# An order of steps for each unit, joint sums of h, and one add moved to GpSimd, in a fused attention and expert kernel

## The chip, the cores and the metric

The kernel runs on one core of one Trainium2 chip. The core has five engines with a queue of instructions each: TensorE (PE; its weight loads are shown as PEld) multiplies matrices and writes to PSUM, eight banks of 512 float32 words in each of 128 partitions; VectorE (DVE), ScalarE (ACT) and GpSimd (POOL) do elementwise work, and SyncE (SP) issues DMAs. Each queue is worked off in order, and engines wait for one another by semaphores. The metric is the device time of one execution in microseconds (us), as the median of several.

## The reference

What is computed is a linear attention with exponential features, whose output is the input of eight experts with a balanced, dense routing:

```python
def phi(x):
    proj = np.einsum('bhsd,df->bhsf', x, w_phi)
    proj = proj - np.max(np.abs(proj), axis=-1, keepdims=True)
    return np.concatenate([np.exp(proj), np.exp(-proj)], axis=-1)
q_p, k_p = phi(q), phi(k)                      # q, k, v: 8 x 8 x 576 x 64
kv = np.einsum('bhsf,bhsd->bhfd', k_p, v)
num = np.einsum('bhsf,bhfd->bhsd', q_p, kv)
den = np.einsum('bhsf,bhf->bhs', q_p, np.sum(k_p, axis=2))[..., None] + 1e-06
x = (num / den), heads side by side            # 4608 x 512
P = routing(x @ w_gate)                        # 4608 x 8, eight rounds of normalising
out = sum over e of P[:, e:e+1] * (relu(x @ w1[e]) @ w2[e])   # w1: 512 x 1024, w2: 1024 x 512
```

All inputs and the output are float32; the kernel multiplies in bfloat16.

## The kernel before

**Stages.** Attention comes first, with the up and down products of expert 0 mixed into it and into the routing, to 244 us. Then come the experts 1 to 7 (`for e in range(1, E)`, near the end of the function), then a short end with the last down products.

**Groups, pairs, units.** The 4608 tokens are nine groups of 512 (g = 0 to 8); groups 0 and 1, 2 and 3, and so on form pairs, group 8 is single. For each expert the loop runs over the four pairs and the single group (in expert 7 the single one first), and for a pair over two halves of the hidden features (fp = 0, 1). Each round of this inner loop is a unit: nine to an expert. A unit has an up part (x @ w1 and relu, of its own groups) and a down part (h @ w2) of one group whose h was completed earlier. An h of a group is two tiles H[0], H[1], one from each fp, which lie in one of six slots of the tile `hs`. The downs lag behind: a pair is complete after its fp = 1 unit, its first group's down is part of the next unit, and its second group's down part of the one after that.

**Products of Strassen's kind.** Up and down are 2 x 2 block products done with seven multiplications (`up7`, `down7`), so sums of blocks have to be made on DVE: `sums_up` and `sums_down` for the weights, `sums_x` for x (kept in DRAM and loaded again for each expert), and in `down7` four sums of the h blocks of each fp, 512 elements a partition each (`sub`, L1239). They go to the tiles S0, S1, S2 (buffers `hx`), and one in place into h. Steps X1, Y1, Z1, X2, X3, Z2, X4 are the seven down products, eight matmuls of 256 columns each (L1462). Their results are scaled by P and added to `acc`, by DVE from PSUM (L1840) or by ACT into a tile V (L1852) and then GpSimd (L1855).

**Fine products.** In experts 2 to 7 the pairs' up part is `up49`: two of its seven products, y (block 12 of w1 with block 21 of x: product two) and w, are themselves done with seven multiplications (`fine`, L1603), in steps a, b, c, d and k. Step a copies one partial product to a tile m5 (kept in xT, ACT, L1615); step b adds m5 to a second partial product (DVE, L1624); the last function, `last` (L1638), adds m5 to the second half of bank 1. For y this add is made in place in PSUM, at the start of step yk, and then `add` (L1664, with relu) forms two blocks of h from y's two banks and k1, the float32 copy of product x1 (ACT `keep`, L1660).

**The order of the work.** A unit's steps are called in the order of a list: `EARLY` for the pairs of expert 1, `FINE[2]` for a single group, and for fine units `FINE[0]` (fp = 1), `FINE[1]` (fp = 0 of an expert's first pair) or `FINE[3]` (other fp = 0). The lists are priorities only: each step calls `pe`, `act`, `dve`, `pool` or `dma`, which enter an operation in a plan. `Plan.schedule` then simulates all engines with costs of its own and takes, each time, the operation that can start first, and of equal ones the one entered first; the queues of the chip get this order. GpSimd's operations and those of DVE marked `shared` (the sums) never overlap in the plan, and a GpSimd operation planned shortly behind such a DVE one gets a wait for it.

**Loads.** X blocks for a pair are loaded by `load_fine` (L1393, SP's queue), into six places for plain blocks and four for fine ones, used in turn; a load waits until the last matmul that reads the place is done. In expert 7 the stores of the output go through the same queue.

Of the kernel before, what the change touches and what calls it, by code (L numbers as in the profile page):

```python
# [12 lines left out]
ALU = mybir.AluOpType  # L13
# [336 lines left out]
def kernel(  # L350
# [650 lines left out]
    def akey(g):  # L1001
        return ["late"] * (g >= NA) + ["P"] * (g >= 9)
# [568 lines left out]
    def up49(A, fp, X, H, gs, r0):  # L1571
# [16 lines left out]
        def fine(bank, an, xn, more=(), takes=(), wk=(), out_c=None):  # L1588

            f, r = A[an]  # L1590
            s, rs = A[an + "*"]
            t, rt = X[xn]
            r = r + rs + rt + list(r0)
            m5, key, first = M5.next()

            def a(q, k):
                return lambda: f()[:, k, 128 * (2 * fp + q):][:, 0:128]

            def sf(n):
                return lambda: s()[:, n, fp, :]  # L1600

            def mul(q, n, lhs, rhs, more=(), takes=(), start=False, wk=()):
                pe(256, lambda: nc.tensor.matmul(  # L1603
                    halves_of(bank[q], n)(), lhsT=lhs(), rhs=t()[:, rhs, :], start=start,
                    stop=True, skip_group_check=True), r + list(more), [bank[q], *wk], takes)

            def copy(q, n, q2, n2):
                act(293, lambda: nc.scalar.copy(
                    out=halves_of(bank[q], n)(), in_=halves_of(bank[q2], n2)()),
                    [bank[q2]], [bank[q]])  # L1610

            def a1():
                mul(1, 0, sf(0), 3, more, takes, True, wk)
                mul(1, 1, a(0, 0), 0)
                act(256, lambda: nc.scalar.copy(out=m5(), in_=halves_of(bank[1], 0)()),  # L1615
                    [bank[1]], [key, *first])
                act(293, lambda: nc.scalar.copy(
                    out=halves_of(bank[0], 0)(), in_=halves_of(bank[1], 1)()),
                    [bank[1]], [bank[0]])

            def a2():
                mul(1, 1, sf(1), 4)
                mul(0, 0, a(0, 1), 1)
                dve(256, lambda: nc.vector.tensor_tensor(  # L1624
                    out=halves_of(bank[0], 1)(), in0=halves_of(bank[1], 1)(), in1=m5(),
                    op=ALU.add), [bank[1], key], [bank[0]])

            def a3():
                mul(1, 1, sf(2), 5)
                mul(0, 1, sf(3), 2)  # L1630
                if out_c is None:
                    copy(1, 0, 1, 1)

            def a4():
                mul(1, 0, a(1, 1), 6, start=out_c is not None)

            def last(out_=None, w=None):
                dve(256, lambda: nc.vector.tensor_tensor(  # L1638
                    out=out_() if out_ else halves_of(bank[1], 1)(),
                    in0=halves_of(bank[1], 1)(), in1=m5(), op=ALU.add),  # L1640
                    [bank[1], key] if out_ else [key], [w] if out_ else [bank[1]])

            return a1, a2, a3, a4, last
# [63 lines left out]
                        [y[q]])  # L1707

        def yk():
            ys[4]()  # L1710
            for q in range(2):
                add(y, q, k1, 1, 1)

# [66 lines left out]
    def down7(e, g, H, B7):  # L1780
# [5 lines left out]
        def hk(i, j, fps=(0, 1)):  # L1786
            return [(H[fp], q, j, i) for fp in fps for q in range(2)]

        late, seen = akey(g), set()
        S = [new(f"S{i}") for i in range(3)]  # L1790
        for fp in range(2):
            def h(i, j, fp=fp):
                return lambda: H[fp]()[:, j, :, 256 * i:256 * i + 256]

            def s(n, fp=fp):
                return lambda: S[n]()[:, 2 * fp:2 * fp + 2]

            f = (fp,)
            end0 = ["dn0"] if e == 1 else []
            sub(dve, 512, s(0), h(1, 0), h(1, 1), ALU.add, hk(1, 0, f) + hk(1, 1, f) + end0,  # L1800
                [(S[0], fp)])
            sub(dve, 512, h(1, 0), h(0, 0), h(1, 0), ALU.subtract, hk(0, 0, f), hk(1, 0, f))
            sub(dve, 512, s(1), s(0), h(0, 0), ALU.subtract,
                [(S[0], fp)] + hk(0, 0, f), [(S[1], fp)])
            sub(dve, 512, s(2), h(0, 1), s(1), ALU.subtract,
                [(S[1], fp)] + hk(0, 1, f), [(S[2], fp)])

        def sk(n):
            return [(S[n], fp) for fp in range(2)]
# [4 lines left out]
        def prod(bank, lhs, y, r, first, more=(), wk=()):  # L1814
            f, r2 = B7[y]
            product(bank, lambda k, i: lhs(k)[:, 128 * i:128 * i + 128],
                    lambda k: f()[:, k, :], 4, r + r2 + (["P"] if e else late) + list(more), first,
                    wk=wk)

        def start(bank, i, j):  # L1820

            out_ = acc_part(g, i, j)
            w = [("acc", g, 2 * i + n, j) for n in range(2)]
            if (i, j) in seen:
                dve(515, lambda: nc.vector.tensor_tensor(
                    out=out_(), in0=bank().rearrange("p (a b) -> p a b", a=2), in1=out_(),
                    op=ALU.add), [bank] + late, w)
            else:
                act(512, lambda: nc.scalar.copy(
                    out=out_(), in_=bank().rearrange("p (a b) -> p a b", a=2)),  # L1830
                    [bank] + late, w)
            seen.add((i, j))

        def read(bank, i, j):
# [62 lines left out]
        def stores():  # L1897
            if e == E - 1:
# [3 lines left out]
        return {"out": stores, "X1": X1, "Y1": Y1, "Z1": Z1, "X2": X2, "X3": X3, "Z2": Z2, "X4": X4}  # L1902


    EARLY = ("X1 x10 w10 x11 X2 x20 y10 x21 Z1 y11 X3 w11 x30 x31 x40 x41 w20 Y1 w21 X4 Z2").split()
    END = "X1 p2 Y1 X2 Z1 p3 X3 Z2 X4 p0 p1".split()
    FINE = [("x11 wa X1 wb wc Z1 X2 wd x10 Z2 ya wk yb x20 x30 yc x21 x31 X3 yd yk w21 x40 x41 Y1 X4 "
             "w20").split(),
            ("X1 ya yb Z1 X2 x11 wa yc wb Z2 X3 Y1 wc wd x10 yd X4 x20 wk x21 yk x30 x31 w20 x40 x41 "
             "w21").split(),  # L1910
            ("x11 y11 x10 x21 w11 Z1 X1 X2 y10 w10 x31 X3 x20 w21 Y1 X4 x41 x30 x40 w20 Z2").split(),
            ("wa wb x11 wc Z1 X1 x10 ya yb yc Z2 x20 wd X2 yd wk X3 x30 yk w20 x21 x40 x31 X4 Y1 w21 "
             "x41").split()]
    slots, wait = list(range(6)), []

    def take():
# [18 lines left out]
    for e in range(1, E):  # L1935
        w1, w2 = load_w(e, ["late", ("acc", 4, 0, 0)] if e > 1 else ["late"])
        if e == 1:
            nextX = sums_x(pairs[0])
        A7 = sums_up(e, w1)
        B7 = sums_down(e, w2) if e > 1 else None  # L1940
        turn = [*pairs, (8,)] if e < E - 1 else [(8,), *pairs]
        if e == 2:
            o = plan.op("X", 0.0, 0.0, lambda: None, w=["K"])
            for d in plan.ops[:-1]:
                if any(b.ring is R["X"] for b in d.bufs):
                    d.users.append(o)
                    o.deps.append(d)
                    o.left += 1
        for n, gs in enumerate(turn):
            if (e, n) == (1, 4):  # L1950
                plan.inorder = 1
            X = nextX if e == 1 else load_fine(gs)
            H = {g: [] for g in gs}
            for fp in range(len(gs)):
                hs = take()
                for i, z in enumerate(hs):
                    H[gs[min(i, len(gs) - 1)]].append(z)
                fine = e > 1 and len(gs) == 2
                if fine:
                    un = up49(A7, fp, X, H, gs, ["up0", "K"])  # L1960
                else:
                    un = up7(A7, gs, fp, X, H, ["up0"])
                single = (e, n) >= (1, 4)
                for o in (FINE[fp == 0 and (1 if n == (e == E - 1) else 3)] if fine else FINE[2] if single else
                          EARLY):
                    if o in un:
                        un[o]()
                    elif len(o) == 3:
                        un[o[:2], int(o[2])]()
                    elif dn is not None:  # L1970
                        dn[o]()
                if dn is not None:
                    dn["out"]()
                    slots.extend(dn["slots"])
                if e == 1 and fp == 0 and n + 1 < len(turn):
                    nextX = sums_x(turn[n + 1], [(H[gs[0]][0], 0, 1, 1)])
                if B7 is None and fp:
                    B7 = sums_down(e, w2)
                if fp == len(gs) - 1:
                    wait += [(e, g, H[g], B7, w2, [z.ring.number for z in H[g]]) for g in gs]  # L1980
                dn = next_down()
# [35 lines left out]
```

## Time and profile before

| | |
|---|---|
| median of 3 runs | 1015.81 us (1015.67 to 1017.01) |
| profiled execution | 1017.14 us, span 1015.4 us |
| PE busy | 999.9 us (98%) |
| PEld busy | 714.1 us (70%) |
| DVE busy | 905.2 us (89%) |
| ACT busy | 770.3 us (76%) |
| POOL busy | 379.6 us (37%) |

The span goes from the first to the last instruction of the profiled execution; its own time has 1.7 us more around that. A busy time is the union of the recorded spans of an engine's instructions, waits not counted. Lines such as L1239 are lines of the kernel, and where a helper makes the instruction it is the helper's line. Rows of groups give the operation, output and inputs by the program's names, shapes, count, then busy time, mean duration, and the idle time before them with what ended it.

### The profile page before, as it was taken

Reading aid. Unit: us, or ns where it says so; the run is one execution under the profiler, and the core shown is the slowest. Engines: PE = TensorE matmul, PEld = TensorE weight load, DVE = VectorE, ACT = ScalarE, POOL = GpSimd, SP = SyncE. Lnnn points to the kernel's source line nnn. Section 1 sums busy time; section 2 is a strip of 40 time slices with the busy share of each in tenths; the row PEclk is TensorE's granted clock in tenths of the full one; section 3 lists DMA queues with packets and bytes.
Section 4 is the critical chain, followed back from the end, with each engine's and each line's share of the span. In section 5 each row is a group of like instructions: output and inputs, shape, how many; then the busy total and the mean of one; then the engine's idle time right before and its main releaser. Section 6 shows DMA issues by size and latency. Waiting matters only on the chain.

```text
span 1015.4 us, 22774 instructions
## 1 busy us (share of the span) xinstructions
PE 999.9 (98%) x8232; PEld 714.1 (70%) x8232; DVE 905.2 (89%) x2075; ACT 770.3 (76%) x1786; POOL 379.6 (37%) x418
## 2 busy tenths in 40 slices
PE   7899999999999999999999999999999999999998
PEld 5666666644576867787777777787778777887775
DVE  7999988987888898999989999899989999988896
ACT  7999999836988777777777677767776777667773
POOL 5778764400123323242333323333342223333323
PEclk9999999999999999999999999999999999999999
DMA  9999999181132622283326333452228222625453
GB/s 251 187 194 184 164 149 132 38 171 47 68 111 74 185 88 89 66 182 100 104 68 143 98 99 98 81 148 89 89 73 203 89 89 66 138 89 150 158 178 125
DMA packets 129681, 123.33 MB, mean 121 GB/s; under 512 B 55712, under 2 KB 98720, under 8 KB 129568
## 3 DMA queue, kind: packets, MB, share of 16 engines
q1 hardware_dynamic: 97616, 97.82, 34.5%
q0 software_dynamic: 31648, 23.86, 16.9%
q8 instruction: 64, 1.05, 0.4%
q14 instruction: 49, 0.40, 0.1%
q10 hardware_dynamic: 304, 0.20, 0.1%
HBM read 117.78 MB, written 18.74 MB: 134 GB/s over the span
## 4 chain that ended last, share of the span: by engine, by line
PE 93%; ACT 3%; DVE 2%; DMA 1%; issue 1%; DVEq 0%; ACTq 0%
PE ps L1462 41%; PE ps L1471 24%; PE ps L621 18%; PE ps L1603 7%; PE ps L904 2%; ACT k L617 1%; DMA xT<-wx 1%; ACT q L617 1%; DMA xT<-xp 0%; ACT acc L1862 0%; DVE m L613 0%; DVE wx L613 0%; PE ps L751 0%; DMA acc<-in_k_dram 0%; PE ps L933 0%
## 5 line engine op out<-in xcount | busy, mean ns | idle before, releaser
L1855 POOL TENSOR_TENSOR acc<-acc,hx 128x512 f32<-128x512 f32 x186 | 235.7, 1271 | 557.9 <-ACT hx L1852 264.9
L1462 PEld LDWEIGHTS <-hs 128*128 128x128 bf16 x1984 | 194.0, 98 | 57.5 <-issue 1.1
L1840 DVE SCALAR_TENSOR_TENSOR acc<-ps,P,acc 128x256 f32<-128x256 f32 x372 | 162.0, 478 | 45.8 <-PE ps L1462 28.5
L1852 ACT ACTIVATE hx<-ps,P 128x256 f32<-128x256 f32 x372 | 156.7, 477 | 48.1 <-PE ps L1462 44.7
L1471 PE MATMUL ps<-xT,T 128*128 128x512 bf16 x608 | 175.8, 379 | 0.8 <-DMA xT<-xp 0.8
L1462 PEld LDWEIGHTS <-hx 128*128 128x128 bf16 x1488 | 145.6, 98 | 27.4 <-issue 0.3
L1462 PE MATMUL ps<-hx,hs 128*128 128x256 bf16 x992 | 141.1, 273 | 0.6 <-ACT hx L1852 0.4
L1664 DVE CUSTOM_DVE_ANT_0 hs<-ps,U 128x512 bf16<-128x512 f32 x192 | 128.7, 683 | 3.5 <-PE ps L1462 1.5
L1471 PEld LDWEIGHTS <-T 128*128 128x128 bf16 x672 | 65.8, 98 | 36.6
L1603 PE MATMUL ps<-xT 128*128 128x256 bf16 x384 | 86.7, 272 | 0.4 <-DVE ps L1624 0.4
L1471 PE MATMUL ps<-xT,wx 128*128 128x512 bf16 x288 | 82.7, 379 | 0.0
L1670 ACT ACTIVATE hs<-ps 128x512 bf16<-128x512 f32 x96 | 57.4, 599 | 29.1 <-PE ps L1471 28.1
L1462 PE MATMUL ps<-wx,hs 128*128 128x256 bf16 x560 | 79.1, 273 | 0.0
L621 PE MATMUL ps<-xT,w 128*128 128x512 bf16 x288 | 72.9, 379 | 0.0
L621 PE MATMUL ps<-w,hx 128*128 128x512 bf16 x288 | 72.6, 379 | 0.0
L1462 PE MATMUL ps<-wx,hx 128*128 128x256 bf16 x496 | 68.5, 273 | 0.0
L1722 ACT COPY ps<-ps 128x512 f32<-128x512 f32 x96 | 53.2, 577 | 20.0 <-DVE acc L1840 16.0
L1462 PE MATMUL ps<-hx 128*128 128x256 bf16 x496 | 68.2, 273 | 0.0
L1664 DVE CUSTOM_DVE_ANT_0 hs<-ps,X 128x512 bf16<-128x512 f32 x96 | 65.2, 683 | 0.5
L613 DVE TENSOR_REDUCE m<-ps 128x4 f32<-128x512 f32 x88 | 58.8, 680 | 3.8 <-PE ps L621 2.0
L1462 PE MATMUL ps<-w,hs 128*128 128x256 bf16 x432 | 61.8, 273 | 0.0
L1660 ACT COPY X<-ps 128x512 f32<-128x512 f32 x96 | 55.9, 597 | 6.1 <-PE ps L1471 6.0
(172 smaller groups left out, 2111.3 us busy)
## 6 DMA issues: line engine op xcount, KB each, us to landing
xT<-xd SPq DMA_DIRECT2D x72, 256.0 KB, 2.7
xT<-xp SPq DMA_DIRECT2D x48, 256.0 KB, 2.7
xT<-xi SPq DMA_DIRECT2D x24, 448.0 KB, 3.6
wx<-in_moe_w_dram POOLq DMA_DIRECT2D x8, 1024.0 KB, 12.4
v_m<-in_v_dram SPq DMA_DIRECT2D x15, 512.0 KB, 5.9
out_dram<-acc SPq DMA_DIRECT2D x14, 512.0 KB, 3.1
w<-in_moe_w_dram POOLq DMA_DIRECT2D x6, 1024.0 KB, 12.4
qk<-in_k_dram POOLq DMA_DIRECT2D x12, 256.0 KB, 5.4
```

What stands on the lines that cost most here:

```text
L613: dve(el, lambda: nc.vector.tensor_reduce(out=dst(), in_=src(), axis=AX.X, op=ALU.max, apply_absolute_value=True), r, w)
L621: nc.tensor.matmul(out_, lhsT=lhsT, rhs=rhs, start=start, stop=stop)
L1462: pe(256, lambda i=i, k=k, z=z: nc.tensor.matmul(bank()[:, 256 * i:256 * i + 256], lhsT=lhs(k, i), rhs=rhs(k), start=first and z, stop=k = ...
L1471: pe(512, lambda k=k: nc.tensor.matmul(bank().rearrange("p (a b) -> p a b", a=2), lhsT=lhs(k), rhs=rhs(k), start=first and k == 0, stop=k ...
L1603: pe(256, lambda: nc.tensor.matmul(halves_of(bank[q], n)(), lhsT=lhs(), rhs=t()[:, rhs, :], start=start, stop=True, skip_group_check=True) ...
L1660: act(512, lambda: nc.scalar.copy(out=flat(to[q])(), in_=bank[q]()), [bank[q]], [(to[q], 0), (to[q], 1)])
L1664: dve(515, lambda: nc.vector._custom_dve(ADD_SAT, out=out_(q, i, j), in0=bank[q]().rearrange("p (a b) -> p a b", a=2), in1=to[q](), s0=3.0 ...
L1670: act(512, lambda: nc.scalar.activation(out=out_(q, i, j), in_=bank[q]().rearrange("p (a b) -> p a b", a=2), func=ACT.Relu, bias=0.0, scal ...
L1722: act(512, lambda: nc.scalar.copy(out=z[q](), in_=x[q]()), [x[q]], [z[q]])
L1840: dve(320, lambda n=n, ts=ts: nc.vector.scalar_tensor_tensor(out=acc[g][:, ts, 256 * j:256 * j + 256], in0=bank()[:, 256 * n:256 * n + 256 ...
L1852: act(370, lambda n=n: nc.scalar.activation(out=u()[:, n, :], in_=bank()[:, 256 * n:256 * n + 256], func=ACT.Copy, bias=0.0, scale=P[:, 4 ...
L1855: pool(695, lambda: nc.gpsimd.tensor_tensor(out=acc[g][:, 2 * i:2 * i + 2, 256 * j:256 * j + 256], in0=acc[g][:, 2 * i:2 * i + 2, 256 * j: ...
```

## The change

Three things are changed.

- Each of an expert's nine units gets a list of its own (`UNITS`, picked by `turns`): lists 0 to 8 for expert 1, 9 to 17 for experts 2 to 6; in expert 7 list 18 for the single group, which comes first there, and then 9 to 16. Every list has the same steps as the one in whose place it stands.
- In `down7`, for experts 2 to 7 and the second group of a pair (g odd) or the single group (`joint`), the four sums of h are made for both fp at once, 1024 elements each, in place of four of 512 for each fp. The operand is a view of `hs` that steps from the one slot to the other.
- In step yk of a fine unit, m5 is no longer added to PSUM by DVE but to the second half of k1's second tile by GpSimd (`later`), in SBUF; `add` then reads the changed k1. Step wk keeps its DVE add.

`own` is the old list `late` of `down7`, renamed.

```diff
--- before.py
+++ after.py
@@ -1634,7 +1634,13 @@
             def a4():
                 mul(1, 0, a(1, 1), 6, start=out_c is not None)
 
-            def last(out_=None, w=None):
+            def later(to, w):
+                pool(330, lambda: nc.gpsimd.tensor_tensor(
+                    out=to(), in0=to(), in1=m5(), op=ALU.add), [key], [w])
+
+            def last(out_=None, w=None, pm=False):
+                if pm:
+                    return later(out_, w)
                 dve(256, lambda: nc.vector.tensor_tensor(
                     out=out_() if out_ else halves_of(bank[1], 1)(),
                     in0=halves_of(bank[1], 1)(), in1=m5(), op=ALU.add),
@@ -1707,7 +1713,7 @@
                         [y[q]])
 
         def yk():
-            ys[4]()
+            ys[4](lambda: k1[1]()[:, 1, :], (k1[1], 1), True)
             for q in range(2):
                 add(y, q, k1, 1, 1)
 
@@ -1786,24 +1792,33 @@
         def hk(i, j, fps=(0, 1)):
             return [(H[fp], q, j, i) for fp in fps for q in range(2)]
 
-        late, seen = akey(g), set()
+        own, seen = akey(g), set()
         S = [new(f"S{i}") for i in range(3)]
-        for fp in range(2):
+        joint = e > 1 and (g % 2 or g == 8)
+        for fp in range(1 if joint else 2):
             def h(i, j, fp=fp):
+                if joint:
+                    def both():
+                        n, m = (z.ring.number for z in H)
+                        return late["hs"][:, n:(m + 1 if m > n else m - 1 if m else None):m - n, j, :,
+                                          256 * i:256 * i + 256]
+                    return both
                 return lambda: H[fp]()[:, j, :, 256 * i:256 * i + 256]
 
             def s(n, fp=fp):
+                if joint:
+                    return lambda: S[n]().rearrange("p (a k) c -> p a k c", a=2)
                 return lambda: S[n]()[:, 2 * fp:2 * fp + 2]
 
-            f = (fp,)
+            def sw(n, fp=fp):
+                return [(S[n], x) for x in ((0, 1) if joint else (fp,))]
+
+            f, el = ((0, 1), 1024) if joint else ((fp,), 512)
             end0 = ["dn0"] if e == 1 else []
-            sub(dve, 512, s(0), h(1, 0), h(1, 1), ALU.add, hk(1, 0, f) + hk(1, 1, f) + end0,
-                [(S[0], fp)])
-            sub(dve, 512, h(1, 0), h(0, 0), h(1, 0), ALU.subtract, hk(0, 0, f), hk(1, 0, f))
-            sub(dve, 512, s(1), s(0), h(0, 0), ALU.subtract,
-                [(S[0], fp)] + hk(0, 0, f), [(S[1], fp)])
-            sub(dve, 512, s(2), h(0, 1), s(1), ALU.subtract,
-                [(S[1], fp)] + hk(0, 1, f), [(S[2], fp)])
+            sub(dve, el, s(0), h(1, 0), h(1, 1), ALU.add, hk(1, 0, f) + hk(1, 1, f) + end0, sw(0))
+            sub(dve, el, h(1, 0), h(0, 0), h(1, 0), ALU.subtract, hk(0, 0, f), hk(1, 0, f))
+            sub(dve, el, s(1), s(0), h(0, 0), ALU.subtract, sw(0) + hk(0, 0, f), sw(1))
+            sub(dve, el, s(2), h(0, 1), s(1), ALU.subtract, sw(1) + hk(0, 1, f), sw(2))
 
         def sk(n):
             return [(S[n], fp) for fp in range(2)]
@@ -1814,7 +1829,7 @@
         def prod(bank, lhs, y, r, first, more=(), wk=()):
             f, r2 = B7[y]
             product(bank, lambda k, i: lhs(k)[:, 128 * i:128 * i + 128],
-                    lambda k: f()[:, k, :], 4, r + r2 + (["P"] if e else late) + list(more), first,
+                    lambda k: f()[:, k, :], 4, r + r2 + (["P"] if e else own) + list(more), first,
                     wk=wk)
 
         def start(bank, i, j):
@@ -1824,11 +1839,11 @@
             if (i, j) in seen:
                 dve(515, lambda: nc.vector.tensor_tensor(
                     out=out_(), in0=bank().rearrange("p (a b) -> p a b", a=2), in1=out_(),
-                    op=ALU.add), [bank] + late, w)
+                    op=ALU.add), [bank] + own, w)
             else:
                 act(512, lambda: nc.scalar.copy(
                     out=out_(), in_=bank().rearrange("p (a b) -> p a b", a=2)),
-                    [bank] + late, w)
+                    [bank] + own, w)
             seen.add((i, j))
 
         def read(bank, i, j):
@@ -1902,15 +1917,39 @@
         return {"out": stores, "X1": X1, "Y1": Y1, "Z1": Z1, "X2": X2, "X3": X3, "Z2": Z2, "X4": X4}
 
 
-    EARLY = ("X1 x10 w10 x11 X2 x20 y10 x21 Z1 y11 X3 w11 x30 x31 x40 x41 w20 Y1 w21 X4 Z2").split()
     END = "X1 p2 Y1 X2 Z1 p3 X3 Z2 X4 p0 p1".split()
-    FINE = [("x11 wa X1 wb wc Z1 X2 wd x10 Z2 ya wk yb x20 x30 yc x21 x31 X3 yd yk w21 x40 x41 Y1 X4 "
-             "w20").split(),
-            ("X1 ya yb Z1 X2 x11 wa yc wb Z2 X3 Y1 wc wd x10 yd X4 x20 wk x21 yk x30 x31 w20 x40 x41 "
-             "w21").split(),
-            ("x11 y11 x10 x21 w11 Z1 X1 X2 y10 w10 x31 X3 x20 w21 Y1 X4 x41 x30 x40 w20 Z2").split(),
-            ("wa wb x11 wc Z1 X1 x10 ya yb yc Z2 x20 wd X2 yd wk X3 x30 yk w20 x21 x40 x31 X4 Y1 w21 "
-             "x41").split()]
+    UNITS = [o.split() for o in (
+        "X1 x10 Y1 Z1 y10 w10 x20 x30 x11 Z2 X2 x40 w11 x21 w21 X3 x31 y11 X4 w20 x41",
+        "w10 Z1 x10 x20 x30 X1 X2 w20 x11 X3 Y1 x21 w11 y11 x31 x41 w21 x40 y10 X4 Z2",
+        "x10 w11 X1 X2 x20 x11 w10 w20 y11 x21 Z1 X3 Y1 x31 w21 x30 y10 X4 x40 Z2 x41",
+        "X1 Y1 w11 Z1 w10 x10 x20 X2 x11 y11 Z2 X3 x21 X4 x31 w21 x41 x30 y10 x40 w20",
+        "x10 X1 w10 x11 w11 Z1 x21 x20 w20 X2 X3 Y1 y11 x30 X4 x31 y10 x40 Z2 x41 w21",
+        "x11 Z1 X1 x21 w11 X2 w10 Y1 x10 x20 y11 Z2 x31 w20 X3 x30 x40 X4 x41 y10 w21",
+        "x10 x20 Z1 X1 x11 Z2 w10 w11 x21 x31 X2 Y1 y10 X3 x30 x40 y11 w21 x41 w20 X4",
+        "x10 X1 Z1 X2 X3 w10 x11 x21 x20 w11 y10 x30 y11 w21 x40 x31 X4 Z2 Y1 x41 w20",
+        "X1 x10 x11 w11 Y1 y10 X2 Z1 X3 w10 x21 y11 x20 x31 x30 w21 Z2 x41 x40 w20 X4",
+        "x10 Z1 wa X1 wb x11 wc wd Z2 X2 x20 X3 wk x21 x30 x31 ya Y1 yb x40 yc yd w21 x41 "
+        "X4 yk w20",
+        "wa x11 wb X1 X2 wc Z1 x10 wd x21 wk x20 x30 Z2 Y1 w21 ya x31 x41 X3 yb w20 yc x40 "
+        "X4 yd yk",
+        "x10 wa wb wc x11 Z1 ya wd X1 yb x20 Z2 wk x21 x31 x41 x30 X2 w21 Y1 yc w20 X3 yd "
+        "yk x40 X4",
+        "x11 x21 wa X1 x10 wb wc ya x20 Y1 wd X2 Z1 wk X3 yb yc yd Z2 w20 x31 yk x30 w21 "
+        "x41 X4 x40",
+        "x11 x21 wa wb Z1 Z2 X1 x10 X2 X3 Y1 wc x20 wd wk w21 x30 x40 ya yb yc x31 X4 w20 "
+        "yd x41 yk",
+        "x11 X1 wa wb wc x10 Z1 ya yb X2 Z2 x20 wd X3 yc x21 wk w20 x31 x30 x40 X4 x41 yd "
+        "yk w21 Y1",
+        "ya wa yb yc Z1 yd Z2 wb wc x10 x11 wd X1 X2 wk x21 yk x20 x31 Y1 X3 w20 x41 x30 X4 "
+        "x40 w21",
+        "ya wa X1 x10 wb yb x11 wc wd X2 yc x20 x21 wk yd Z1 Z2 X3 w21 x31 x41 x30 w20 x40 "
+        "X4 Y1 yk",
+        "x11 w10 x10 w11 X1 X2 X3 x20 y11 x21 Z1 x30 w20 y10 X4 Y1 w21 x40 Z2 x31 x41",
+        "x10 X1 x11 y10 w11 X2 x20 w10 x21 Z1 Z2 x31 X3 x41 X4 Y1 w21 y11 x30 x40 w20")]
+    turns = [int(i) for i in (
+        "0 1 2 3 4 5 6 7 8 9 10 11 12 13 14 15 16 17 9 10 11 12 13 14 15 16 17 9 10 11 12 "
+        "13 14 15 16 17 9 10 11 12 13 14 15 16 17 9 10 11 12 13 14 15 16 17 18 9 10 11 12 "
+        "13 14 15 16").split()]
     slots, wait = list(range(6)), []
 
     def take():
@@ -1960,9 +1999,7 @@
                     un = up49(A7, fp, X, H, gs, ["up0", "K"])
                 else:
                     un = up7(A7, gs, fp, X, H, ["up0"])
-                single = (e, n) >= (1, 4)
-                for o in (FINE[fp == 0 and (1 if n == (e == E - 1) else 3)] if fine else FINE[2] if single else
-                          EARLY):
+                for o in UNITS[turns.pop(0)]:
                     if o in un:
                         un[o]()
                     elif len(o) == 3:
```

## The prediction

> **What bounds the kernel now.** I read the page's busy line first, then the table of windows by stage, then the waits of TensorE, then the rows of the instructions that the change touches, and last the timeline at two places. The page and the row of the granted clock:
>
> ```profile
> PE 999.9 (98%) x8232; PEld 714.1 (70%) x8232; DVE 905.2 (89%) x2075; ACT 770.3 (76%) x1786; POOL 379.6 (37%) x418
> ...
> PEclk9999999999999999999999999999999999999999
> ```
>
> TensorE has work all the time, at full granted clock. The windows, one per stage, have length, then the busy time of PE, PEld, DVE, ACT and POOL. Experts two to six run from 349 to 890, expert seven follows:
>
> ```profile
> 0.00:50.00 50.00, 40.92 (x417) 28.80 (x418) 44.38 (x93) 44.54 (x112) 32.69 (x61) 1.00 1.17 218
> ...
> 244.00:349.30 105.30, 104.86 (x715) 69.74 (x713) 85.34 (x201) 89.81 (x178) 28.09 (x23) 1.00 0.41 116
> 349.30:457.50 108.20, 107.79 (x830) 81.00 (x829) 98.15 (x226) 79.18 (x185) 35.85 (x29) 1.00 0.38 100
> 457.50:565.70 108.20, 108.20 (x835) 81.45 (x833) 99.95 (x228) 78.65 (x186) 35.88 (x29) 1.00 0.39 107
> ...
> 890.00:1001.00 111.00, 110.19 (x848) 82.61 (x846) 97.31 (x218) 79.61 (x189) 34.22 (x27) 1.00 0.41 131
> ```
>
> See that the large hole (9 us) lies in the first 50 us, where nothing of the change runs, and that from 244 us on, where all of it runs, PE idles under 1 us in 100. The waits of PE from 244 us to the end are these four alone:
>
> ```profile
> PE ps L1471 <- DMA xT<-xp: 0.8, 1, 0.8
> PE ps L1462 <- ACT hx L1852: 0.4, 1, 0.4
> PE ps L1603 <- DVE ps L1624: 0.4, 1, 0.4
> PE ps L1462 <- DVE acc L1840: 0.2, 1, 0.2
> ```
>
> A matmul's recorded end lies after the start of the next, so short waits hide. I therefore took the starts of successive matmuls: one of 256 columns follows the one before after 0.109 us, one of 512 after 0.216; what goes beyond is a wait. **The ledger from 244 us on is 4.5 us**: behind DVE 2.7 (six times 0.15 at the fine products' add L1624 and 0.07 just ahead of it, once an expert, at 422, 530, 639, 747, 855 and 953 us, 1.3 together; 0.58 at 356.6; 0.36 at 763.1; 0.31 at 610; 0.12 at 1000.1), behind a DMA 0.97 at 935.3, behind ACT 0.8 in expert one. That is the most that this change can bring: it removes no matmul, and 244 us of attention and the end (last matmul at 1011.6, span 1015.4) stay as they are.
>
> **The change part by part.** Rows, with duration minimum/median/maximum in ns:
>
> ```profile
> L1638 DVE TENSOR_TENSOR ps<-ps,xT x48: 421/423/433, 357.8 to 995.8; 128x256 f32<-128x256 f32 x48
> ...
> L1239 DVE TENSOR_TENSOR hx<-hs x108: 412/419/1442, 349.6 to 997.5; 128x512 bf16<-128x512 bf16 x108
> ...
> L1239 DVE TENSOR_TENSOR hx<-hx,hs x108: 411/417/1469, 352.8 to 998.3; 128x512 bf16<-128x512 bf16 x108
> ...
> L1239 DVE TENSOR_TENSOR T<-wx x7: 682/684/686, 445.4 to 891.2; 128x1024 bf16<-128x1024 bf16 x7
> ...
> L1855 POOL TENSOR_TENSOR acc<-acc,hx x163: 1262/1271/1282, 350.9 to 1001.2; 128x512 f32<-128x512 f32 x163
> ```
>
> *Joint h sums.* There are 62 downs with seven products; 29 of them (experts two to seven, second group of each pair and the single group, without the one that the end computes plainly) get four sums of 1024 in place of eight of 512. In a row, 512 elements take 0.335 us from start to start (two sums span 0.75 in the timeline, less one duration of 0.42) and 1024 take 0.60: 8 x 0.335 - 4 x 0.60 = 0.28 us, 29 times, **8 us less on DVE**. The new sums step over two h slots; the nearest row, 1024 elements in strided blocks of xT, takes the same 0.69. If the stride cost the packed rate, a sum would go at the rate of L1638 (0.33 us for 256, so 1.3 for 1024, 82 us more on DVE); below 0.60 no row goes. I take 0.60. The joint sum waits for both halves of h, but these groups' h are complete a whole unit (12 us) before: cost nothing; where the split sums of the first group begin before the second half is there, they stay split.
>
> *Product two's last term.* 48 DVE adds go (pitch 0.33 us: **16 us less on DVE**); 48 GpSimd adds of 256 come. Between half of L1855 (0.64) and all of it (1.27), nearer to half: 0.7, 34 us, **GpSimd 380 to 413 us**, of which 6 us per expert beside 36 of 108: not on the path. It can start when k1's copy and m5 are there, both at the product's begin; the DVE adds to h come after its last matmul, some us later, and PSUM is left 0.33 us earlier. Behind it in GpSimd's queue stand the acc adds L1855 and two weight loads an expert (one issue 0.84): each may come 0.7 later. An acc add frees a V tile for the next scaled copy (ACT L1852), which frees a bank; ACT now waits 0.2 us in all for that after 349 us, so the cover is the 72% of the time in which GpSimd is idle. In expert seven the stores in SP's queue wait for acc adds, and the X loads stand behind the stores: there 0.7 us may pass on to the wait at 935.
>
> *Port.* GpSimd's adds collide with the sums, which both read SBUF twice. In the timeline, one expert's first sum that meets an acc add:
>
> ```profile
> 432.19 1.27 POOL L1855 TENSOR_TENSOR acc<-acc,hx 128x512 f32<-128x512 f32 x1 [1.60 <-ACT hx L1852]
> 432.27 1.47 DVE L1239 TENSOR_TENSOR hx<-hx,hs 128x512 bf16<-128x512 bf16 x1
> ```
>
> The sum takes 1.47 instead of 0.42, and the ledger has no wait of PE there or in the next 50 us: **1 us of lateness of DVE is covered**. The other DVE forms (L1840, L1664, L1638) take the same time with and without GpSimd beside them. The Trainium skill (SBUF — State Buffer, "Who interferes with whom") has the rule: a DVE instruction with two SBUF inputs and a GpSimd one that reads SBUF exclude each other for the whole instruction, and it speaks against this change, which trades 48 adds with a PSUM input (free of it) for 48 on GpSimd. The trace agrees with it. By that rule each of the 48 that met a sum would cost 0.7 us of DVE, 34 us at worst, against 24 saved.
>
> *The 19 orders.* Each holds the same steps as the list that it replaces (21 or 27), so no matmul, copy or DMA is added. What moves is which wait falls where. The X loads on SP's queue are issued when the tile's last reader is done: the tightest that I find is the block "22" of the third pair, freed by x40, now the last step of the unit before, and needed at w21, sixteenth step, some 7.7 us of matmuls later; a load lands in 2.7, so 5 us are left (before: about 8). Steps of a fine product that stand side by side and must be filled by the planner are as many as before: "b c" 7 times an expert in both, "a b" 5 for 7, but "c d" 3 for 0. So I give the orders no sum of their own beyond the ledger, bounded by -4.5 us and, upward, by one repeated wait the size of the largest DVE one (0.58, six times: +3.5).
>
> *Sum.* DVE has 24 us less, 4 an expert; of the ledger I take the part that DVE ends, 2.7 us, as gone or nearly (**-2.6**), and leave the DMA's 0.97 and ACT's 0.8, which nothing here relieves. The profiled execution took 1017.1 (span 1015.4 and 1.7 around), 1.3 above the median of 1015.81; it would be 1014.5, and **the median 1013.2**.
>
> **The rivals.** *One: waits only change places.* The repeated 0.15 is a chain of one add between two matmuls, behind a sum in DVE's order, not a lack of DVE time (DVE's own pitch fills 92 of 108 us). New orders make other such places: within 2 us of 1015.8, say 1015.3. For it: the equal number of neighbouring steps. Against: DVE's load does fall.
>
> *Two, slower: GpSimd holds DVE up.* At the end of product two DVE's in-order queue must wait for the GpSimd add; if that add stands behind an acc add it comes 1.27 + 0.7 = 2.0 us after its cause, and all PSUM reads behind wait. It decides from the 1 us that is covered: one such unit per expert gives 1.0 us x 6, 1022; two, 1028. Against it: GpSimd idles 72%, and the add is ready early.
>
> *Three, slower: one new place in the units that recur.* A wait of 0.58 in one of nine units, six times, over an otherwise unchanged ledger: 1019.3. The DMA margin of 5 us in the third pair, lost to the stores in expert seven, would add 1 to 2.
>
> *Four:* the strided joint sums do not get the packed rate: 14 us an expert on DVE less 2.6 from GpSimd's adds, 92 becomes 103 of 108, PE stalled here and there: about 1025.
>
> **How the numbers follow.** What a measurement of this kernel can tell from no change is 0.2%, 2.0 us. Forecast (over 2 us faster) 0.42; rival one 0.33; two 0.10, three 0.12, four 0.03, together slower 0.25. The range begins at 1011.3, the whole ledger gone (0.04 below), and reaches to 1019.3, the price of rival three, beyond which I leave rivals two, four and a little of three (0.15). The forecast's own range is 1011.3 to 1013.8.
>
> **What would show it.** DVE busy near 881, GpSimd near 413; L1638 on ps gone; four joint sums at 0.69 a down; the six waits at L1624 missing from PE's starts. Wrong if PE gains a wait that recurs every 108 us, if DVE waits for GpSimd's new add, or if sums of 1.4 us and more number well over the present dozen with PE idle behind them.

## The result and the profile after

The changed kernel takes 1012.96 us (median of 6 runs, 1012.18 to 1013.51) against 1016.67 of the kernel before on the same chip (1015.67 to 1017.12): a ratio of 0.9965, 95% interval 0.9952 to 0.9978, 3.7 us less. The profiled execution took 1013.5 us with a span of 1011.7, before 1017.1 and 1015.4. The forecast was 2.6 us less, with 1011.3 to 1019.3 as the range.

The page after, busy time and share of the span:

```profile
PE 997.0 (99%) x8232; PEld 712.1 (70%) x8232; DVE 879.9 (87%) x1911; ACT 771.8 (76%) x1786; POOL 412.9 (41%) x466
```

The windows of the changed kernel, for the same stretches as before (the last one ends earlier, as expert seven does), columns as before:

```profile
244.00:349.30 105.30, 105.30 (x718) 69.96 (x717) 87.49 (x203) 89.95 (x181) 28.14 (x23) 1.00 0.42 116
349.30:457.50 108.20, 108.20 (x836) 81.34 (x834) 94.65 (x203) 79.16 (x188) 41.44 (x37) 1.00 0.37 100
457.50:565.70 108.20, 108.14 (x835) 81.34 (x833) 95.20 (x199) 78.99 (x187) 41.43 (x37) 1.00 0.39 107
890.00:998.00 108.00, 108.00 (x828) 80.60 (x826) 92.48 (x188) 77.58 (x183) 39.71 (x35) 1.00 0.41 134
```

See that TensorE is busy through these windows but for 0.06 us, where up to 0.8 us of a window was missing before, and that an expert's stretch has some 25 DVE instructions and 4 us of DVE less, and 8 GpSimd instructions more. The only wait of TensorE that the profile still lists from 244 us on is this:

```profile
PE ps L1603 <- DVE ps L1624: 0.2, 1, 0.2
```

By the starts of successive matmuls, the measure of the prediction, the ledger after 244 us fell from 4.5 to 0.7 us (0.34 at 854.3, 0.23 at 558.8, three of 0.06 and less in expert one). That is 3.8 us, as much as the whole gain; attention takes as long as before (the first up product of expert one, L1471, starts at 244.2 us, before at 244.1). The rows of the two moved pieces of work, durations minimum/median/maximum in ns:

```profile
L1638 POOL TENSOR_TENSOR X<-X,xT x48: 718/726/737, 358.0 to 986.4; 128x256 f32<-128x256 f32 x48
...
L1239 DVE TENSOR_TENSOR hs<-hs x79: 414/426/693, 350.0 to 995.5; 128x512 bf16<-128x512 bf16 x50, 128x1024 bf16<-128x1024 bf16 x29
```

GpSimd's add of 256 takes 0.73 us. Of this kind of sum 29 are joint and 50 split, and none took more than 0.69, what a sum of 1024 without that step took before (0.68 to 0.69): the step from slot to slot costs nothing.

### The profile page after: what moved, and what is told of

Read it like the earlier page. It is cut to its first block, busy times and chain, and to the rows that moved or that the text cites. A ratio compares the mean times of both kernels' runs of the same rounds, so it can differ in the third digit from the quotient of the medians.

```text
span 1011.7 us, 22631 instructions
## 1 busy us (share of the span) xinstructions
PE 997.0 (99%) x8232; PEld 712.1 (70%) x8232; DVE 879.9 (87%) x1911; ACT 771.8 (76%) x1786; POOL 412.9 (41%) x466
## 3 DMA queue, kind: packets, MB, share of 16 engines
q8 instruction: 64, 1.05, 0.4%
## 4 chain that ended last, share of the span: by engine, by line
PE 94%; DMA 2%; ACT 2%; DVE 1%; issue 0%; SPq 0%; DVEq 0%
PE ps L1462 42%; PE ps L1471 25%; PE ps L621 18%; PE ps L1603 7%; PE ps L904 2%; DMA acc<-in_q_dram 1%; DMA xT<-wx 1%; ACT q L617 1%; ACT k L617 1%; DVE wx L613 0%; PE ps L751 0%; ACT wx L617 0%; PE ps L933 0%; DVE m L613 0%; DVE ps L912 0%
## 5 line engine op out<-in xcount | busy, mean ns | idle before, releaser
L1471 PE MATMUL ps<-xT,T 128*128 128x512 bf16 x608 | 179.1, 379 | 0.0
L1462 PE MATMUL ps<-hx,hs 128*128 128x256 bf16 x992 | 134.8, 273 | 0.1
L1471 PEld LDWEIGHTS <-T 128*128 128x128 bf16 x672 | 65.6, 98 | 36.0
L1471 PE MATMUL ps<-xT,wx 128*128 128x512 bf16 x288 | 84.1, 379 | 0.0
L1462 PE MATMUL ps<-wx,hs 128*128 128x256 bf16 x560 | 76.9, 273 | 0.0
L1638 POOL TENSOR_TENSOR X<-X,xT 128x256 f32<-128x256 f32 x48 | 34.9, 726 | 91.2 <-DVE hx L1239 34.3
## 6 DMA issues: line engine op xcount, KB each, us to landing
wx<-in_moe_w_dram POOLq DMA_DIRECT2D x8, 1024.0 KB, 12.8
```

What stands on the lines that cost most here:

```text
L1462: pe(256, lambda i=i, k=k, z=z: nc.tensor.matmul(bank()[:, 256 * i:256 * i + 256], lhsT=lhs(k, i), rhs=rhs(k), start=first and z, stop=k = ...
L1471: pe(512, lambda k=k: nc.tensor.matmul(bank().rearrange("p (a b) -> p a b", a=2), lhsT=lhs(k), rhs=rhs(k), start=first and k == 0, stop=k ...
```

## The experiments

In all that follows "ledger" is the sum of TensorE's waits of over 20 ns after 244 us, from the starts of matmuls. The profiles of some runs lack the records of 36 matmuls; their weight loads are all there, and those gaps were allowed for. Ratios are to the kernel before on the same chip, with the 95% interval.

Two theories stood at the start besides the prediction's own (A, DVE's relief ends the waits that DVE ended): the places of the steps decide and DVE's load is nothing (B), and the orders fit only the lighter DVE (C).

### The three edits, apart and by twos

The orders alone, that is the changed kernel without its two edits of work:

```diff
-        joint = e > 1 and (g % 2 or g == 8)
+        joint = False
...
-            ys[4](lambda: k1[1]()[:, 1, :], (k1[1], 1), True)
+            ys[4]()
```

> The 19 orders, with the split sums and product two's last add on DVE as before. Theory A (the waits that DVE ended went because DVE has 24 us less): the orders take away only the waits of the DMA and of ACT, 1.8 of the 4.5 us of the ledger after 244 us; time 0.2% under before. Theory B (the places of the steps decide, DVE's load is nothing): ledger under 1 us as in the changed kernel, time 0.35% under before. Theory C (the orders fit only the lighter DVE): new repeated waits, ledger over 4.5 us, no faster than before.

The two edits alone, with the old lists:

```diff
...   # the lists EARLY and FINE stand again in the place of UNITS and turns
-                for o in UNITS[turns.pop(0)]:
+                single = (e, n) >= (1, 4)
+                for o in (FINE[fp == 0 and (1 if n == (e == E - 1) else 3)] if fine else FINE[2] if single else
+                          EARLY):
```

> The joint sums and the GpSimd add, with the old orders. Theory A: the 2.7 us of waits that DVE ended are gone, those of the DMA (0.97) and of ACT (0.8) stay: ledger 1.8 us, time 0.25% under before. Theory B: the same kind of waits at the same places or others, ledger 3 to 6 us, time within 0.1% of before. Theory C says the same as B, or worse.

The orders with the joint sums (only the second part of the first diff), and the orders with the GpSimd add (only its first part):

> The 19 orders and the joint sums, product two's last add on DVE in PSUM as before (8 of the 24 us less on DVE). Theory A: between orders alone and the whole change, ledger 1 to 1.5 us. Theory B: ledger under 1 us, time as the whole change. Theory C: some repeated waits behind product two, ledger 2 to 5 us.

> The 19 orders and the GpSimd add, sums split as before (16 of the 24 us less on DVE). Theory A: ledger about 1 us. Theory B: under 1 us, time as the whole change. Theory C: some repeated waits behind the sums at a unit's begin, ledger 2 to 4 us.

After these, each edit of work alone with the old lists:

> The joint sums alone, old orders (DVE 8 us less). What the first four runs left standing is that the DVE work taken away brings nothing under the old orders. So: within 0.15% of before, ledger after 244 us between 4 and 5 us. If instead this edit costs by itself (its sums hold both slots longer): ledger over 6.

> The GpSimd add alone, old orders (DVE 16 us less, GpSimd 35 us more). As for the joint sums alone: within 0.15% of before, ledger 4 to 5 us. If GpSimd's adds hold DVE up (rival two of the prediction): waits of PE behind the second h add of product two, ledger over 6.

| orders | joint sums | GpSimd add | ratio to before | ledger, us |
|---|---|---|---|---|
| old | no | no | 1 | 4.5 |
| old | yes | no | 1.0014 (1.0005 to 1.0023) | 6.5 |
| old | no | yes | 1.0012 (1.0003 to 1.0021) | 5.7 |
| old | yes | yes | 1.0010 (1.0001 to 1.0018) | 4.4 |
| new | no | no | 1.0159 (1.0145 to 1.0172) | 19.8 |
| new | yes | no | 1.0057 (1.0044 to 1.0069) | 10.0 |
| new | no | yes | 1.0099 (1.0085 to 1.0113) | 14.1 |
| new | yes | yes | 0.9965 (0.9952 to 0.9978) | 0.7 |

Of the seven variants six are no faster than before, and only all three edits together are. The orders alone cost 16 us, the edits of work alone gain nothing, and with the new orders each edit is worth 6 to 14 us. Theory C stands, A and B fall; but C's sizes for the orders with one edit, 2 to 5 us of ledger, were far too small (10.0 and 14.1). What these runs leave open is whether an order found anew for the old work would bring as much: none was run.

The ledgers of the two single edits missed the expected 4 to 5 us: 6.5 with the joint sums, of which DVE ends 4.4, and 5.7 with the GpSimd add, of which ACT ends 4.5. By the sign that was set for it (over 6), the joint sums cost something by themselves under the old orders; by what stays open. The wait of 0.15 us at L1624, once an expert before, stands at eleven places with the joint sums alone and at none with the GpSimd add, alone or with the joint sums: it goes with the moved add, and other waits come.

Waits of TensorE from 244 us on, with the orders alone:

```profile
PE ps L1462 <- ACT ps L1886: 3.9, 11, 0.4
PE ps L1603 <- DVE ps L1624: 1.9, 5, 0.8
PE ps L1603 <- ACT ps L1617: 1.6, 8, 0.3
PE ps L1471 <- ACT X L1666: 1.0, 4, 0.2
PE ps L1603 <- ACT ps L1608: 0.4, 1, 0.4
```

They recur every 111 us: in expert four the ledger has 1.7 us between 593 and 603, 0.59 at 627.6 and 1.0 between 646 and 652, and the 0.59 stands again at 516.4, 738.7 and 849.8. One of them, in the timeline of the same run:

```profile
602.46 0.10 PEld L1603 LDWEIGHTS <-w 128*128 128x128 bf16 x1
602.55 0.57 ACT L1886 COPY ps<-ps 128x512 f32<-128x512 f32 x1 [0.63 <-PE ps L1462]
602.57 0.27 PE L1603 MATMUL ps<-xT,w 128*128 128x256 bf16 x1
...
603.17 0.71 PE L1462 MATMUL ps<-hx 128*128 128x256 bf16 x5 [0.33 <-ACT ps L1886]
```

ACT copies the product X1 to the bank in which Y1 or X2 goes on; the steps stand so close that a single matmul of fill (602.57) lies between, and TensorE waits out the copy. With the two edits and the old orders the waits are others than before, but not less:

```profile
PE ps L1471 <- DMA xT<-xd: 1.0, 1, 1.0
PE ps L1603 <- DVE ps L1624: 0.6, 2, 0.4
PE ps L1462 <- ACT hx L1867: 0.4, 1, 0.4
PE ps L1462 <- DVE acc L1855: 0.2, 1, 0.2
PE ps L1471 <- ACT X L1666: 0.2, 1, 0.2
```

By the ledger, DVE ended 1.5 us of them (before 2.7), ACT 1.7 (0.8), a DMA 1.1 (1.0). In these eight kernels a DMA's wait stands under the old orders only; none of the four with the new ones has it.

### Load on the chip, or the order that the plan makes of it

An edit acts in two ways: DVE has less to do on the chip, and the plan, told so, puts all queues in another order. Two experiments part them. In the first the plan knows nothing: the second h add of product two is issued twice in each fine unit, on DVE, in the changed kernel and in the one before.

```diff
-            dve(515, lambda: nc.vector._custom_dve(...), ...)
+            dve(515, lambda: [one() for _ in range(times)][0], ...)   # one() issues the add
...
-                add(y, q, k1, 1, 1)
+                add(y, q, k1, 1, 1, 1 + 1 * q)
```

> The changed kernel, with the second h add of product two issued twice on DVE in each fine unit, which the plan does not know of: every queue has the same order, and DVE 48 x 0.6 = 29 us more work, more than the 24 that the change takes away. Theory C1 (the new orders need a DVE that is light on the chip): ledger 15 to 20 us, time 1.4 to 1.7% over the changed kernel, as with the orders alone. Theory C2 (what fails without the two edits is the order that the plan works out for heavier costs, not the load on the chip): DVE's 19 idle us an expert cover it, ledger under 4 us, time within 0.3% of the changed kernel.

> The same doubled add in the kernel before. C1: the old orders have more cover, so less is lost than in the changed kernel, 2 to 8 us. C2: little is lost, as in the changed kernel, under 3 us.

The traces show a dearer add than the 0.60 us expected. The copy writes the same place as the first add (0.68 us), starts 0.71 to 0.73 us after it, when it has ended, and 48 of them are 34 us. DVE's busy time rose by 30.0 us to 909.8, in the kernel before by 28.6 to 933.8.

The changed kernel went to 1.0140 (1.0124 to 1.0155) of before, ledger 19.0: 17.7 us lost. The kernel before went to 1.0258 (1.0244 to 1.0272), ledger 30.1: 26 us lost, where 2 to 8 us (C1) or under 3 (C2) had been expected. The old orders have less cover against such work, not more. Waits of TensorE in the changed kernel with the doubled add:

```profile
PE ps L1471 <- DVE hs L1671: 6.2, 20, 0.5
PE ps L1462 <- DVE acc L1858: 1.8, 6, 0.3
PE ps L1603 <- DVE ps L1624: 1.5, 5, 0.3
PE ps L1462 <- DVE hs L1671: 1.0, 4, 0.3
PE ps L1462 <- DVE hx L1239: 0.2, 1, 0.2
```

In the second the chip's work is that of the changed kernel, but the plan is told the old durations:

```diff
-            f, el = ((0, 1), 1024) if joint else ((fp,), 512)
+            f, el = ((0, 1), 1158) if joint else ((fp,), 512)
...
-                add(y, q, k1, 1, 1)
+                add(y, q, k1, 1, 1, 832 if q == 0 else 515)    # elements that the plan counts
```

> The changed kernel does the same work on the chip, but the plan is told the old costs: 0.075 us more for each joint sum and 0.33 us more for the first h add of product two, 4 us of DVE an expert. Theory C1 (a heavy DVE on the chip stalls PE): the chip is light, so the ledger after 244 us stays under 3 us and the time within 0.2% of the changed kernel. Theory C2 (the plan's order for heavier costs loses the time): ledger 8 to 20 us, as with the orders alone, time 0.7 to 1.9% over the changed kernel.

The time was 1.0086 (1.0071 to 1.0100) of before, the ledger 12.8, and these are the waits of TensorE:

```profile
PE ps L1462 <- ACT ps L1886: 2.2, 5, 0.4
PE ps L1603 <- ACT ps L1617: 1.0, 5, 0.2
PE ps L1471 <- ACT ps L1728: 0.4, 1, 0.4
```

So C1 (the load on the chip) and C2 (the plan's order) are both true, each strong enough alone: 5.7 us of DVE an expert lose 18 us when they come on the chip unplanned, and 4 us an expert lose 12 when they are only in the plan. The engine that ends TensorE's waits differs: with the doubled add DVE ends 18.7 of the 19.0 us of the ledger, with the old durations in the plan ACT ends 12.0 of 12.8, and the orders alone, which have both, look like the second kind (15.0 of 19.8 for ACT). It is no general mark: with the joint sums alone, where the plan has another order and DVE less work, DVE ends 4.4 of 6.5. What the plan's order has to do with ACT, which no edit touches, stays open: the runs show the lines, not why the plan leaves these steps side by side.

Does the place of the late DVE work matter? The first of the four h sums was made twice in each down of experts two to seven:

```diff
-            sub(dve, el, s(0), h(1, 0), h(1, 1), ALU.add, hk(1, 0, f) + hk(1, 1, f) + end0, sw(0))
+            dve(el * 0.5, twice, hk(1, 0, f) + hk(1, 1, f) + end0, sw(0), shared=True)   # twice() issues it twice
```

> The changed kernel with the first of the four h sums issued twice in every down of experts two to seven, unknown to the plan: 29 x 0.60 + 48 x 0.335 = 33 us more on DVE, at another place than the doubled h add of product two (29 us, 18 us lost). If DVE's total load decides: ledger about 20 us, 1.7 to 2.1% over the changed kernel. If the place decides: the sums stand in the idle stretches of DVE at a unit's begin, with up to 1 us of cover as the collisions showed, ledger under 8 us, less than 0.8% over.

1.0167 (1.0153 to 1.0181), ledger 21.2, DVE ending 16.8 of it and ACT 4.5: 20.5 us lost, 2.0% over the changed kernel, as expected if the load decides. The 33 us expected for the sums are too few. The second of two split sums starts 0.46 us after the first, and 16 of the joint ones, which meet a GpSimd instruction, take longer than the usual 0.69; by starts it is some 48 us, and DVE's busy time rose by 38.7. Each added microsecond of busy time so costs TensorE 0.5 us here, 0.6 with the doubled add (17.7 / 30.0), and 0.9 in the kernel before (26 / 28.6). The two places pay nearly alike.

### GpSimd's add made late

One and four copies of 256 elements, which write back what they read, were put ahead of each moved add, in GpSimd's queue and unknown to the plan; by the rows each takes 0.46 to 0.47 us.

```diff
+                def go():
+                    first = [nc.gpsimd.tensor_copy(out=to(), in_=to()) for _ in range(4)]   # or range(1)
+                    return (first + [nc.gpsimd.tensor_tensor(out=to(), in0=to(), in1=m5(), op=ALU.add)])[0]
```

> The changed kernel with one extra copy of 256 on GpSimd ahead of each moved add (0.3 to 0.7 us, unknown to the plan). In the trace of the changed kernel the second h add of product two starts 0.4 us (one unit of eight), 1.5 us (two) or 2.8 to 8.9 us (five) after the end of GpSimd's add. Cover theory: only the 0.4 us unit can be touched, at most 0.3 us x 6; ledger under 3 us, within 0.2% of the changed kernel. Rival two of the prediction (every lateness of GpSimd goes on to DVE): 48 x 0.4, over 1%.

> The same with four extra copies, some 1.2 to 2.6 us late. Cover theory: the units with 0.4 and 1.5 us of room are late by 1 to 2 us in all of their second h adds, an expert loses 1 to 3.5 us, six of them 6 to 20 us; the five roomy units lose nothing. Rival two: all 48 are late, 60 us and more.

One copy: 0.9987 (0.9978 to 0.9996), 0.2% over the changed kernel, ledger 2.6. The size is the one expected, its place is not: five waits of 0.22 to 0.24 behind ACT (L1732) and six of 0.12 to 0.13 behind DVE (L1624) make up the 1.9 us more, and none of them follows the add of the unit with 0.4 us of room (behind the one at 423.9 the next wait is at 487). Four: 1.0102 (1.0087 to 1.0116), ledger 15.1, 14 us over. In the trace of the second, DVE's h add starts right when GpSimd's add ends (0.03 us) in two of the eight fine units of an expert, the seventh and eighth, the two with 0.4 and 1.5 us of room, and 2.1 us or more after it in the other six (but for the first unit of expert two, 0.03, and one of expert seven, 0.95). Such a place in the timeline:

```profile
647.47 0.73 POOL L1640 TENSOR_TENSOR X<-X,xT 128x256 f32<-128x256 f32 x1
648.22 0.37 ACT L1615 COPY xT<-ps 128x256 f32<-128x256 f32 x1 [0.55 <-POOL X L1640]
648.23 0.69 DVE L1674 CUSTOM_DVE_ANT_0 hs<-ps,X 128x512 bf16<-128x512 f32 x1 [1.40 <-POOL X L1640]
...
649.43 0.87 DVE L1859 SCALAR_TENSOR_TENSOR acc<-ps,P,acc 128x256 f32<-128x256 f32 x2
...
650.35 0.81 PE L1462 MATMUL ps<-hx,hs 128*128 128x256 bf16 x6 [1.08 <-DVE acc L1859]
```

DVE stands 1.40 us for GpSimd, ACT 0.55 (the next unit's m5 may not be written before GpSimd has read this one), and behind a sum and the two adds to `acc` TensorE stands 1.08 for DVE. By starts this wait is 1.24 us, and it comes once in each of experts two to seven (0.89 in expert six). So the cover theory holds for the seventh unit, whose add is 1.5 us later than its room, and for the roomy ones at this place; in the eighth, 0.4 us later than its room, DVE stands for GpSimd and TensorE does not wait.

That is half of the loss. In experts two to six another 1.3 us stands in units whose own add has room (0.76 at 595 and 0.51 at 605 us in expert four). The copies also put off the acc adds that stand behind them in GpSimd's queue, and these now meet DVE's sums:

```profile
592.11 1.27 POOL L1874 TENSOR_TENSOR acc<-acc,hx 128x512 f32<-128x512 f32 x1
592.23 1.70 DVE L1239 TENSOR_TENSOR hx<-w,hx 128x1024 bf16<-128x1024 bf16 x1
...
595.31 0.38 PE L1603 MATMUL ps<-xT 128*128 128x256 bf16 x2 [0.60 <-DVE ps L1624]
```

In the changed kernel this weight sum took 0.68 us (at 587.40); here it takes 1.0 more, and TensorE waits 0.76 behind the DVE instructions that follow. Ahead of 605 a joint h sum takes 1.30 for 0.68 in the same way. So lateness on GpSimd has a second road to TensorE, past the units with room; it is read from the timelines, and no run takes the collisions away.

## Why the prediction was right or wrong

**The bound.** Right: with 4.5 us in the ledger the change could bring no more, and it brought 3.7, the ledger 3.8. That this is little in 1016 us could be read from the starts of the matmuls; the four listed waits, 1.8 us, show less than half of it.

**The prices of the work.** Right one by one: GpSimd rose by 33.3 us (34 forecast), the moved add takes 0.73 (0.7), a joint sum 0.68 to 0.69 where it meets no GpSimd work. Rival four, the lost packed rate, did not come. That DVE's total fell by 25.3 us, close to the 24 forecast, is partly luck. With the old orders the two edits take 20.2 us from it. And 9.7 of the 25.3 are collisions with GpSimd, which the sum did not count: after 349 us, sums over 0.1 us longer than their kind had 12.5 us too much in the kernel before (16 sums) and 2.9 in the changed one (12). The moved add brings collisions under the old orders (19.4 us in 40 sums with that edit alone), not under the new ones, so that the worst case of 34 us stayed far off. In the changed kernel they are mostly joint sums of 0.89 to 0.97 us, and the ledger has no wait right behind them.

**The sum.** Its size was near (-2.6 forecast, -3.7 measured), its reason was wrong: the number came out by luck, and two steps of it failed. The first is "of the ledger I take the part that DVE ends, 2.7 us, as gone or nearly", because DVE has 24 us less: with the old orders that relief ends 1.2 us of these waits, puts nearly as many on ACT and the DMA, and the time is 0.1% longer. The second is "I give the orders no sum of their own": the orders have by far the largest, +16 us alone, and -4.6 us (from 1.0010 to 0.9965) on top of the two edits. With both edits they end nearly all waits, the DMA's 0.97 and half of ACT's 0.8 among them, which the sum had kept; 0.34 us behind DVE and 0.34 behind ACT are left.

**The cover.** "1 us of lateness of DVE is covered", read from one sum that stood 1.05 us for GpSimd, is wrong as a general price: 0.71 us unplanned in each fine unit costs TensorE 0.54 us in the kernel before and 0.37 in the one after, and the collision at 592.23 above, 1.0 us, costs 0.76. The reading took a wait that the plan itself holds free for GpSimd (a shared DVE operation is planned behind it, by the code of `start`) for a lateness. That explanation rests on the code; no run took it apart.

**The rivals.** One, "waits only change places", is what the edits of work do under the old orders (ledger 4.4 for 4.5). Its argument that the repeated 0.15 us is "not a lack of DVE time" is neither shown nor refuted for this wait, which outlasts the joint sums and goes with the moved add, the larger relief; that DVE has time to spare is refuted by the doubled add and the doubled sum. Two, GpSimd holding up DVE, has the right mechanism: made 1.9 us late, the add holds DVE up in two units an expert, and TensorE pays 1.24 us for one of them, near the 1.0 that the rival took. As built, the tightest unit has 0.4 us of room, and nothing is paid. Three, one new place that recurs, did not come with the whole change; it is what comes, several times over, under the new orders as soon as one of the other edits is left out. Two readings of the prediction are off without a bearing on its sum: GpSimd idled 67% of an expert, not 72 (36 of 108 us were busy), and "c d" stand side by side once in an expert's old lists and four times in the new, not 0 and 3.

## What to carry to other kernels

An engine that idles 15% of its time beside a saturated one has no slack by that alone: when queues are fixed beforehand and each bank of PSUM is handed on just in time, ask what an added microsecond on it costs, by issuing an instruction of it twice, and read from the trace how much time that adds. An order found for one set of durations belongs to it: price changes of work and of order together, and do not judge either by undoing the other. Whether a new search for an order alone would do, only such a search can say. And take the bound of a gain from the waits of the saturated engine before anything else; here it gave the size even where the reason was wrong.

## What the runs showed that was not expected

DVE's instructions, counted by their distance when they follow at once, fill some 92 of 108 us an expert before and 89 after, and still a microsecond more of its busy time costs 0.9 us before and 0.5 to 0.6 after, at the two places tried. The GpSimd add takes 0.73 us for 256 elements where 512 take 1.27: 0.54 for the second 256, so, if both halves cost alike, 0.19 us does not depend on the size (an estimate from these two rows).
